# Attention scores with keys on partitions, no row maximum, and the old program kept behind a branch

## The chip, the cores and the metric

The kernel runs on one core of a Trainium2 chip. The core has a matrix engine (TensorE; its matmuls are called PE and its weight loads PEld in the profile), a vector engine (VectorE, DVE), a scalar engine (ScalarE, ACT), a general engine (GpSimd, POOL) and a queue engine (SyncE, SP) which starts the DMAs here. Each runs its own list of instructions in order, and semaphores hold one back until another has delivered. SBUF is the memory on chip, of 128 partitions; matmuls write to PSUM. The metric is the device time of one execution in microseconds (us), lower is better.

## What is computed

```python
# q, k, v: (4, 8, 768, 64), proj: (64, 6), w_in: (512, 2048), w_out: (2048, 512), alpha: (2048,)
q_bits = (np.einsum('bhsd,dk->bhsk', q, proj) > 0)      # the same for k
q_bucket = np.sum(q_bits * 2 ** np.arange(6), axis=-1)  # the same for k
mask = q_bucket[:, :, :, None] == k_bucket[:, :, None, :]
scores = scale * np.matmul(q, k.transpose(0, 1, 3, 2))
scores = np.where(mask, scores, -1000000000.0)
scores = scores - np.max(scores, axis=-1, keepdims=True)
attn = np.exp(scores)
attn = attn / (np.sum(attn, axis=-1, keepdims=True) + 1e-09)
x = (attn @ v).transpose(0, 2, 1, 3).reshape(3072, 512)
h = x @ w_in
g = np.maximum(h, 0.0) + alpha * np.minimum(h, 0.0)
out = g @ w_out
```

q, k and v are normal numbers times 0.1. The weights come as float64 and are rounded to float32 on chip. A query without any key in its bucket attends to all keys alike.

## The kernel before

Heads go in pairs, one on partitions 0 to 63, the other on 64 to 127; there are 4 batches of 4 pairs. A step (`scores`, L188) takes 128 queries of a pair against all 768 keys. The queries are on partitions. A bf16 matmul of the hash bits (`kb`, `qb`) puts 0 where the buckets are equal and a large negative number elsewhere, and the fp32 matmul of `kT` and `qT` adds the scores onto it in PSUM (L195). VectorE clamps the row and takes its maximum (L204, L207), ScalarE takes the exponentials and their sum (L209), and GpSimd divides by the sum (L219). The product with v needs the weights with keys on partitions, so `turn_probs` (L222) turns them on TensorE, 128 by 128 at a time (tile `pp`, L229), ScalarE copies them back (`pt`, L233), and `attend` (L235) multiplies with v (L242).

A batch has 24 steps, the program 96. The first 16 steps also each round one of sixteen half weight tiles (`round_weight`, L141: two passes on ScalarE, five on VectorE, L151 to L159, one on GpSimd, L158), loaded two ahead into two buffers. From step 26 on the MLP of the batch before is spread between the steps (`mlp_slice`, L288): `ff1` (L251, tile `h`, then two VectorE operations into `g`) and `ff2` (L265, tile `z`). The last batch's MLP runs alone after the attention has ended. A step turns, hashes and prepares the next pair as well (`turn`, L164; `hash_bits`, L175). The engines' lists follow this order, except that the scheduler moves an instruction forward where the operands of the next one in its list are late. An fp32 matmul stands as one row in the order and as two passes, each with a weight load of its own, in the profile.

PSUM has 8 banks: two for `tp`, used by all small products, two for `ff`, and two for the scores of each head.

Of the kernel before, what the change touches and what calls it, by code (L numbers as in the profile page):

```python
# [8 lines left out]
F32 = mybir.dt.float32  # L9
BF16 = mybir.dt.bfloat16  # L10
# [6 lines left out]
def kernel(  # L17
# [11 lines left out]
    """Hash-bucketed attention, then the PReLU MLP, all in float32.  # L29

    Heads go in pairs (head A on partitions 0-63, head B on 64-127). Token 6p + c of a
    sequence sits at column 128c + p throughout, so that loads and stores have long runs.
    Queries lie on partitions for the softmax; the weights are turned on the tensor
    engine, and v^T @ P^T gives x already transposed for the first MLP product.

    Bucket mask: with bits in {0, 1},
        sum_i (qb_i - 1/2) * 2*BIG*kb_i - BIG*qb_i = -BIG * (number of unequal bits),
    a matmul of powers of two that is exactly 0 for equal buckets. The scores are added
    onto it in PSUM, and max(., CLAMP) makes every masked entry the reference's -1e9
    (before the scale), so a row without any equal bucket becomes uniform as there.  # L40

    The MLP weights come as float64 bits; they are rounded to float32 on chip.
    """
# [18 lines left out]
    HI_MIN = 2.0 ** -15                                 # bits 0x38000000: 2^-127 as a float64's upper half  # L62
    HI_MAX = (2.0 - 2.0 ** -3 - 2.0 ** -23) * 2.0 ** 16  # bits 0x47EFFFFF: just below 2^128
# [77 lines left out]
    def round_weight(i):  # L141
        """hi, lo: the halves of a float64. Its exponent is moved to float32's range by
# [92 lines left out]
    def attend(pi, g):  # L235
# [4 lines left out]
        for kc in range(NC):  # L240
            for s in range(2):
# [3 lines left out]
                )  # L245
        nc.vector.tensor_copy(xT[b][:, hp, g * 2 * P : (g + 1) * 2 * P], ps)  # L246

# [1 line left out]
    gT, z, mpool = {}, {}, []  # L249

    def ff1(b, ch, f):  # L251
# [124 lines left out]
```

## Time and profile before

| | |
|---|---|
| median of 3 runs | 1307.92 us (1305.82 to 1308.66) |
| the profiled execution, span | 1303.8 us |
| granted TensorE clock, mean | 0.975 |
| HBM read, written | 35.67 MB, 6.29 MB |

In the profile, a group is one line's instructions of one kind: what they write and read, the shape, how many, the busy time and the mean of one, then the idle time of the engine just before them and what ended it. "64*128" is the part of the array that a matmul or a weight load takes, in rows and columns. Matmuls overlap with the next, so that the spacing of their starts tells what one costs, and not its mean length.

### The profile page before, as it was taken

How to read it: one execution, taken by the hardware profiler on the slowest of the kernel's cores; microseconds unless marked ns; L12 is line 12 of the kernel's file. 1: busy time of each engine (PE TensorE's matmuls, PEld its weight loads, DVE VectorE, ACT ScalarE, POOL GpSimd, SP SyncE). 2: the span in 40 equal slices, each digit the busy share in tenths (PEclk: the TensorE clock that was granted, in tenths of full speed). 3: DMA queues.
4: the chain of work that ended last, by engine and by line, in shares of the span. 5: the costliest groups of instructions: out<-in, count | busy, mean ns of one | idle time of the engine just before them, and what ended most of it. 6: DMA issues, size and time to landing. Idle time of an engine off the chain costs nothing.

```text
span 1303.8 us, 14044 instructions
## 1 busy us (share of the span) xinstructions
PE 1247.5 (96%) x5569; PEld 669.4 (51%) x5569; DVE 516.0 (40%) x1140; ACT 414.5 (32%) x793; POOL 222.8 (17%) x214
## 2 busy tenths in 40 slices
PE   6778899999999999999999999999999999999998
PEld 3444455555545555555555554555545555554553
DVE  5877654454215432244223442244323441040230
ACT  3665545433223323233232332323323233100000
POOL 2643532211111111111111111111111111000000
PEclk8997789999999999999999999999999999999999
DMA  8343301101010010101001010100000000000000
GB/s 216 111 156 107 122 13 37 37 1 37 9 34 19 1 37 17 45 1 25 21 9 45 1 37 9 41 13 13 1 17 9 1 1 9 17 1 16 9 0 25
DMA packets 62755, 42.87 MB, mean 33 GB/s; under 512 B 51408, under 2 KB 55520, under 8 KB 62688
## 3 DMA queue, kind: packets, MB, share of 16 engines
q1 hardware_dynamic: 62688, 41.97, 11.1%
q8 instruction: 44, 0.72, 0.2%
q14 instruction: 23, 0.19, 0.0%
HBM read 35.67 MB, written 6.29 MB: 32 GB/s over the span
## 4 chain that ended last, share of the span: by engine, by line
PE 74%; DVE 12%; ACT 7%; issue 3%; POOL 2%; SPq 1%; DMA 0%; ACTq 0%; POOLq 0%; DVEq 0%
PE z L271 26%; PE h L255 15%; PE sc L195 12%; PE av L242 9%; PE pp L229 7%; DVE pr L204 7%; ACT pr L209 5%; ACT pt L233 2%; PE hs_k L181 2%; PE hs_q L181 1%; POOL wr L158 1%; POOL pr L219 1%; DVE nm L207 1%; PE tp_k L172 1%; DVE wr L156 1%
## 5 line engine op out<-in xcount | busy, mean ns | idle before, releaser
L255 PE MATMUL h<-xT,w_in 128*128 128x384 f32 x1024 | 361.2, 492 | 0.0
L271 PE MATMUL z<-w_out,g 128*128 128x512 f32 x768 | 349.8, 597 | 0.0
L209 ACT ACTIVATE pr<-pr,nm 128x768 f32<-128x768 f32 x192 | 178.0, 928 | 500.0 <-DVE nm L207 500.0
L219 POOL TENSOR_SCALAR pr<-pr,rs 128x768 f32<-128x768 f32 x192 | 184.8, 974 | 809.4 <-DVE rs L217 529.9
L204 DVE TENSOR_SCALAR_CACHE_REDUCE pr<-sc 128x768 f32<-128x768 f32 x192 | 176.6, 953 | 188.5 <-PE sc L195 188.5
L255 PEld LDWEIGHTS h<-xT,w_in 128*128 128x128 f32 x1024 | 184.2, 190 | 117.5 <-issue 14.6
L271 PEld LDWEIGHTS z<-w_out,g 128*128 128x128 f32 x768 | 139.3, 190 | 152.7 <-issue 148.2
L229 PEld LDWEIGHTS pp<-ident,pr 128*128 128x128 f32 x1152 | 134.6, 144 | 131.8 <-ACT pt L233 60.1
L229 PE MATMUL pp<-ident,pr 128*128 128x128 f32 x1152 | 170.0, 284 | 33.5 <-ACT pt L233 15.8
L233 ACT COPY pt<-pp 128x512 f32<-128x512 f32 x288 | 158.4, 582 | 97.2 <-PE pp L229 96.0
L195 PE MATMUL sc<-kT,qT 64*128 64x512 f32 (+1 forms) x768 | 185.0, 509 | 0.0
L260 DVE TENSOR_SCALAR neg<-h,alpha 128x384 f32<-128x384 f32 x128 | 79.1, 618 | 227.6 <-PE h L255 227.5
L242 PE MATMUL av<-pt,vn 128*64 128x256 f32 x1152 | 138.8, 388 | 2.8 <-ACT pt L233 2.8
L242 PEld LDWEIGHTS av<-pt,vn 128*64 128x64 f32 x1152 | 79.8, 139 | 48.8 <-ACT pt L233 9.2
L195 PEld LDWEIGHTS sc<-kT,qT 64*128 64x128 f32 x768 | 77.9, 198 | 42.0 <-issue 39.1
L195 PE MATMUL sc<-kb,qb 64*128 64x256 bf16 (+1 forms) x384 | 79.7, 339 | 8.2 <-DVE pr L204 7.8
L277 ACT COPY o<-z 128x512 f32<-128x512 f32 x24 | 13.9, 580 | 220.0 <-PE z L271 220.0
L246 DVE COPY xT<-av 128x256 f32<-128x256 f32 x48 | 20.3, 422 | 152.2 <-PE av L242 152.1
L262 DVE SCALAR_TENSOR_TENSOR g<-h,neg 128x384 f32<-128x384 f32 x128 | 71.4, 558 | 4.3
L195 PEld LDWEIGHTS <-qb 64*128 64x128 bf16 x384 | 22.4, 94 | 85.0 <-issue 83.9
L216 DVE TENSOR_SCALAR rs<-rs 128x2 f32<-128x2 f32 x96 | 19.2, 200 | 93.3 <-ACT pr L209 92.6
L158 POOL TENSOR_TENSOR wr<-wx,wr 128x1024 f32<-128x1024 f32 x16 | 37.7, 2354 | 74.8 <-ACT wx L150 22.2
(46 smaller groups left out, 415.1 us busy)
## 6 DMA issues: line engine op xcount, KB each, us to landing
raw<-in_moe_w_in_dram SPq DMA_DIRECT2D x8, 1024.0 KB, 5.2
raw<-in_moe_w_out_dram SPq DMA_DIRECT2D x8, 1024.0 KB, 5.0
qn<-in_q_dram SPq DMA_DIRECT2D x32, 192.0 KB, 3.4
kn<-in_k_dram SPq DMA_DIRECT2D x32, 192.0 KB, 3.3
vn<-in_v_dram SPq DMA_DIRECT2D x16, 384.0 KB, 3.1
out_dram<-o SPq DMA_DIRECT2D x24, 256.0 KB, 2.0
wq<-in_proj_dram SPq DMA_DIRECT2D x2, 1.5 KB, 3.2
wk<-in_proj_dram SPq DMA_DIRECT2D x2, 1.5 KB, 2.1
```

The source lines that it names most:

```text
L158: nc.gpsimd.tensor_tensor(r, x, r, op=ALU.add)
L195: nc.tensor.matmul(sc[s][:, lo:hi], what["q", pi][r, qs], what["k", pi][r, lo:hi], start=first, stop=not first,)
L204: nc.vector.tensor_scalar(pr[:, s], sc[s], CLAMP, None, op0=ALU.max, op1=ALU.max, accum_out=mx[:, s : s + 1],)
L209: nc.scalar.activation(pr[:, s], pr[:, s], AF.Exp, scale=SCALE, bias=nm[:, s : s + 1], accum_out=rs[:, s : s + 1],)
L219: nc.gpsimd.tensor_scalar(pr[:, s], pr[:, s], rs[:, s : s + 1], 1.0, op0=ALU.mult, op1=ALU.mult)
L229: nc.tensor.transpose(ps[:, kk, j * P : (j + 1) * P], prob[pi, 2 * g + j][:, s, (kc + kk) * P : (kc + kk + 1) * P], ident,)
L233: nc.scalar.copy(p[:, kc : kc + 2], ps)
L242: nc.tensor.matmul(ps[D * s : D * s + D], nat["v", pi][:, s, kc * D : (kc + 1) * D], pt[pi, g, s][:, kc], start=(kc == 0), stop=(kc == NC ...
L255: nc.tensor.matmul(ps, w[:, kk, o : o + P], xT[b][:, kk, ch * CW : (ch + 1) * CW], start=(kk == 0), stop=(kk == NK - 1),)
L260: nc.vector.tensor_scalar(neg, ps, 0.0, alpha[:, f : f + 1], op0=ALU.min, op1=ALU.mult)
L262: nc.vector.scalar_tensor_tensor(g, ps, 0.0, neg, op0=ALU.max, op1=ALU.add)
L271: nc.tensor.matmul(ps, gT[b, ch, f][:, t * P : (t + 1) * P], w_out[part][:, i], start=(f == 0), stop=(f == NF - 1),)
```

## The change

The old function is kept, under the name `general_path`. A new `fast_path` runs first and writes the whole output. It also writes a flag, which all five engines read at the end; where it isn't 0, `general_path` computes everything again.

In `fast_path` a unit is 384 queries of a pair, 32 units in all, in four slots each. `scores` takes 128 keys as the stationary operand and 384 queries as the moving one, for both heads into two PSUM banks, so the exponentials come out with keys on partitions. They aren't turned, and no row maximum is taken. `hash_bits` is one product with 64 columns for q and one for k, side by side, and the bits lie on 12 rows of each head in place of 64. The bits' constant is 2^20 in place of 2^34 and the clamp is left out, so that masked entries come out of the exponential as 0. The sum over keys is made by adding the six tiles of exponentials (`acc`), five additions on GpSimd, in the first four pairs the last two of them on VectorE, and by a product with a matrix of ones (`sm`). `attend` multiplies with undivided exponentials; tiles carry a 385th column of ones, with which the mean of v falls out. `divide` multiplies by the reciprocal, and puts the mean of v where the sum is 0. `magnitude` takes the largest and smallest entries of q^T and k^T, and `verdict` makes the flag from them. Two weights are rounded in a unit (8 units), and the MLP starts with unit 9. The `ff1`, `ff2`, `round_weight` and the loads are as before, except that `g` has 18 buffers and not 20.

```diff
-def tile_hash_attn__then__act_prelu_kernel(
+def general_path(
...
+    flag = const_flag = None
+    args = (tc, q, k, v, proj, moe_w_in, moe_w_out, moe_alpha, out)
+    keep = ctx.enter_context(tc.tile_pool(name="keep", bufs=1))
+    flag = keep.tile([1, 1], mybir.dt.int32, name="flag")
+    fast_path(*args, flag)
+    again = tc.nc.values_load(flag[0:1, 0:1])
+    with tc.If(again > 0):
+        general_path(*args)
...
+    BIG = 2.0 ** 20
+    SAFE = 80.0 / SCALE / D
...
+    NPT = 9
+    pts = [const.tile([P, 2, CW + 1], F32, name=f"pt{i}") for i in range(NPT)]
...
+    def turn(pi, name, half):
+        src = nat[name, pi].rearrange("p c h d -> p c (h d)")
+        if half == 0:
+            tr[name, pi] = pool.tile([P, S], F32, name=f"{name}T{pi}", tag=f"{name}T")
+        ps = psum.tile([P, CW], F32, name=f"tp_{name}{pi}{half}", tag="mi")
+        for i in range(CH):
+            nc.tensor.transpose(ps[:, i * P : (i + 1) * P], src[:, CH * half + i], ident)
+        nc.scalar.copy(tr[name, pi][:, half * CW : (half + 1) * CW], ps)
+    def magnitude(pi, name):
+        n = "qk".index(name)
+        for i, op in enumerate((ALU.max, ALU.min)):
+            nc.vector.tensor_reduce(
+                mags[:, n, 2 * pi + i : 2 * pi + i + 1], tr[name, pi], axis=mybir.AxisListType.X, op=op,
+            )
+    def hash_bits(pi, half):
+        if half == 0:
+            for name in "qk":
+                bits[name, pi] = pool.tile([P, S], BF16, name=f"{name}b{pi}", tag=f"{name}b")
+        cols = slice(half * CW, (half + 1) * CW)
+        ps = psum.tile([P, CW], F32, name=f"hs{pi}{half}", tag="mi")
+        for n, name in enumerate("qk"):
+            nc.tensor.matmul(ps[D * n : D * n + D], wh, tr[name, pi][:, cols], start=True, stop=True)
+        for s in range(2):
+            dst = slice(D * s, D * s + 2 * NB)
+            r = slice(32 * s, 32 * s + 2 * NB)
+            nc.vector.tensor_scalar(bits["q", pi][dst, cols], ps[r], 0.0, cq[r], op0=ALU.is_gt, op1=ALU.subtract)
+            r = slice(D + 32 * s, D + 32 * s + 2 * NB)
+            nc.vector.tensor_scalar(bits["k", pi][dst, cols], ps[r], tk[r], mk[r], op0=ALU.is_gt, op1=ALU.mult)
+    def scores(pi, g, part):
+        qs = slice(g * CW, (g + 1) * CW)
+        for kc in (2 * part, 2 * part + 1):
+            sc = psum.tile([P, 2, 512], F32, name=f"sc{pi}_{g}_{kc}", tag="sc")
+            ks = slice(kc * P, (kc + 1) * P)
+            for what, first, rows in ((bits, True, 2 * NB), (tr, False, D)):
+                for s in range(2):
+                    r = slice(D * s, D * s + rows)
+                    nc.tensor.matmul(
+                        sc[:, s, :CW], what["k", pi][r, ks], what["q", pi][r, qs], start=first, stop=not first,
+                    )
+            pt = pts[n_pt[0] % NPT]
+            n_pt[0] += 1
+            nc.scalar.activation(pt[:, :, :CW], sc[:, :, :CW], AF.Exp, scale=SCALE)
+            prob[pi, g, kc] = pt
+            if kc == 1:
+                acc[pi, g] = pool.tile([P, 2, CW], F32, name=f"acc{pi}_{g}", tag="acc")
+            if kc >= 1:
+                a = acc[pi, g]
+                first = prob[pi, g, 0][:, :, :CW] if kc == 1 else a
+                eng = nc.vector if pi < NP and kc >= 4 else nc.gpsimd
+                eng.tensor_tensor(a, first, pt[:, :, :CW], op=ALU.add)
+    def attend(pi, g):
+        ps = psum.tile([P, CW + 1], F32, name=f"av{pi}_{g}", tag="mi")
+        for kc in range(NC):
+            for s in range(2):
+                nc.tensor.matmul(
+                    ps[D * s : D * s + D], nat["v", pi][:, s, kc * D : (kc + 1) * D], prob[pi, g, kc][:, s],
+                    start=(kc == 0), stop=(kc == NC - 1),
+                )
+        if g == 0:
+            vmean[pi] = pool.tile([P, 1], F32, name=f"vm{pi}", tag="vm")
+            nc.vector.tensor_scalar(vmean[pi], ps[:, CW : CW + 1], 1.0 / S, None, op0=ALU.mult)
+        raw_x = pool.tile([P, CW], F32, name=f"rx{pi}_{g}", tag="rx")
+        nc.scalar.copy(raw_x, ps[:, :CW])
+        av[pi, g] = raw_x
+    def divide(pi, g):
+        b, hp = pairs[pi]
+        if hp == 0 and g == 0:
+            xT[b] = pool.tile([P, NP, S], F32, name=f"xT{b}", tag="xT")
+        ps = psum.tile([P, CW], F32, name=f"sm{pi}_{g}", tag="mi")
+        for s in range(2):
+            nc.tensor.matmul(ps[D * s : D * s + D], ones, acc[pi, g][:, s], start=True, stop=True)
+        den = pool.tile([P, CW], F32, name=f"dn{pi}_{g}", tag="dn")
+        alone = pool.tile([P, CW], F32, name=f"al{pi}_{g}", tag="al")
+        x = xT[b][:, hp, g * CW : (g + 1) * CW]
+        nc.vector.tensor_scalar(alone, ps, 0.0, vmean[pi], op0=ALU.is_equal, op1=ALU.mult)
+        nc.vector.tensor_scalar(den, ps, 1e-36, None, op0=ALU.max)
+        nc.vector.reciprocal(den, den)
+        nc.gpsimd.tensor_tensor(den, av[pi, g], den, op=ALU.mult)
+        nc.gpsimd.tensor_tensor(x, den, alone, op=ALU.add)
...
+        g = mpool[0].tile([P, CW], F32, name=f"g{b}_{ch}_{f}", tag="g", bufs=NF + 2)
...
+    def verdict():
+        both = const.tile([P, 2, 2], F32, name="both")
+        for i, op in enumerate((ALU.max, ALU.min)):
+            nc.vector.tensor_reduce(
+                both[:, :, i], mags.rearrange("p n (x t) -> p n x t", t=2)[:, :, :, i],
+                axis=mybir.AxisListType.X, op=op,
+            )
+        top = const.tile([P, 2], F32, name="top")
+        nc.vector.tensor_scalar(both[:, :, 1], both[:, :, 1], -1.0, None, op0=ALU.mult)
+        nc.vector.tensor_tensor(top, both[:, :, 0], both[:, :, 1], op=ALU.max)
+        row = const.tile([1, 2], F32, name="row")
+        for n in range(2):
+            ps = psum.tile([1, P], F32, name=f"vd{n}", tag="mi")
+            nc.tensor.transpose(ps, top[:, n : n + 1], ident)
+            nc.vector.tensor_reduce(row[:, n : n + 1], ps, axis=mybir.AxisListType.X, op=ALU.max)
+        nc.vector.tensor_tensor(row[:, 0:1], row[:, 0:1], row[:, 1:2], op=ALU.mult)
+        nc.vector.tensor_scalar(row[:, 0:1], row[:, 0:1], SAFE, None, op0=ALU.is_le)
+        nc.vector.tensor_scalar(flag, row[:, 0:1], -1.0, 1.0, op0=ALU.mult, op1=ALU.add)
+    UNITS = NP * NCH
+    SLOTS = 4 * UNITS
+    total = NPAIR * NCH
+    def mlp_slice(u, slot):
+        n = 4 * (u - UNITS - 1) + slot
+        if n < 0:
+            return
+        b, i = divmod(n, SLOTS)
+        if b < B:
+            m = mlp[b]
+            for fn, *a in m[len(m) * i // SLOTS : len(m) * (i + 1) // SLOTS]:
+                fn(*a)
+    def ahead(u, slot):
+        pi, g = divmod(u, NCH)
+        if pi + 1 >= NPAIR:
+            return
+        if slot < 2:
+            turn(pi + 1, "qk"[g], slot)
+        elif slot == 2:
+            magnitude(pi + 1, "qk"[g])
+        if g == 1 and slot >= 2:
+            hash_bits(pi + 1, slot - 2)
+    weights = ctx.enter_context(ExitStack())
+    wpool = weights.enter_context(tc.tile_pool(name="wstage", bufs=2))
+    NW = 2 * len(views)
+    load_qk(0)
+    setup()
+    load_v(0)
+    load_qk(1)
+    for name in "qk":
+        for half in range(2):
+            turn(0, name, half)
+        magnitude(0, name)
+    for half in range(2):
+        hash_bits(0, half)
+    setup_alpha()
+    load_v(1)
+    load_weight(0)
+    load_weight(1)
+    for u in range(total + UNITS + 2):
+        pi, g = divmod(u, NCH)
+        live = u < total
+        if u == UNITS:
+            weights.close()
+            mpool.append(ctx.enter_context(tc.tile_pool(name="mlp", bufs=2)))
+        for slot in range(4):
+            if live and slot != 1:
+                scores(pi, g, (0, None, 1, 2)[slot])
+            if live and slot == 0 and g == 0 and pi + 2 < NPAIR:
+                load_qk(pi + 2)
+                load_v(pi + 2)
+            if slot % 2 == 0 and 2 * u + slot // 2 < NW:
+                i = 2 * u + slot // 2
+                round_weight(i)
+                if i + 2 < NW:
+                    load_weight(i + 2)
+            if live:
+                ahead(u, slot)
+            mlp_slice(u, slot)
+            if 0 < u <= total:
+                before = divmod(u - 1, NCH)
+                if slot == 0:
+                    attend(*before)
+                if slot == 2:
+                    divide(*before)
+        if u == total + 1:
+            verdict()
```

TensorE in the mixed stage before, one step of the first MLP batch (`h` is the MLP, `sc` the scores, `pp` the turned probabilities):

```order
L195 LDWEIGHTS qb_1547
L195 MATMUL sc_3_0_1849<-kb_1596,qb_1547 128x512
L195 LDWEIGHTS qb_1547
L195 MATMUL sc_3_1_1850<-kb_1596,qb_1547 128x512
L195 MATMUL sc_3_0_1849<-kT_1478,qT_1425 128x512
L172 MATMUL tp_k_1826<-ident,kn_1347 128x128 x3
L172 MATMUL tp_k_1831<-ident,kn_1347 128x128 x3
L195 MATMUL sc_3_1_1850<-kT_1478,qT_1425 128x512
```

And after, in the mixed stage, between two pieces of the MLP (`sm` is the product that makes the sums; `kb` and `qb` are the bits):

```order
L632 MATMUL h_1_11_2047<-xT_387,w_in_79 128x384 x4
L615 MATMUL sm_1_2056<-acc_1_1798,ones 64x384 x2
L578 LDWEIGHTS kb_1872
L578 MATMUL sc_0_4_2066<-qb_1871,kb_1872 128x384
L578 LDWEIGHTS kb_1872
L578 MATMUL sc_0_4_2066<-qb_1871,kb_1872 128x384
L578 MATMUL sc_0_4_2066<-qT_1685,kT_1800 128x384 x2
L578 LDWEIGHTS kb_1872
L578 MATMUL sc_0_5_2073<-qb_1871,kb_1872 128x384
L578 LDWEIGHTS kb_1872
L578 MATMUL sc_0_5_2073<-qb_1871,kb_1872 128x384
L578 MATMUL sc_0_5_2073<-qT_1685,kT_1800 128x384 x2
```

Keys have become the weights. For each tile of 128 keys the list goes from the bits' 12 rows to the scores' 64 rows and back. Over the whole list the shape of the array changes 599 times in the fast path, 192 of them from a 32-row shape to a 64-row one and 100 straight back; before it changes 362 times.

VectorE in the rounding stage before (`wx`, `wr`, `w_in` belong to a weight, `pr` and `mx` to the row maxima, `nm` and `rs` to the softmax's factors):

```order
L183 TENSOR_SCALAR qb_389<-hs_q_393,cq 128x384
L152 TENSOR_SCALAR wx_419<-wx_419 128x1024
L216 TENSOR_SCALAR rs_4_413<-rs_4_413 128x2
L204 TENSOR_SCALAR pr_5_471,mx_5_472<-sc_5_0_461 128x768
L155 TENSOR_SCALAR wr_420<-wx_419 128x1024
L217 RECIPROCAL rs_4_413<-rs_4_413 128x2
L204 TENSOR_SCALAR pr_5_471,mx_5_472<-sc_5_1_462 128x768
L156 SCALAR_TENSOR_TENSOR wr_420<-raw_286,wr_420 128x1024
```

And after (`mags` are the magnitudes, `al` and `dn` the steps of `divide`):

```order
L526 TENSOR_SCALAR wr_442<-wx_441 128x1024
L526 TENSOR_SCALAR wr_494<-wx_493 128x1024
L527 SCALAR_TENSOR_TENSOR wr_442<-raw_320,wr_442 128x1024
L527 SCALAR_TENSOR_TENSOR wr_494<-raw_374,wr_494 128x1024
L530 SCALAR_TENSOR_TENSOR w_in_79<-raw_320,wr_442 128x1024
L530 SCALAR_TENSOR_TENSOR w_in_79<-raw_374,wr_494 128x1024
L548 TENSOR_REDUCE mags<-qT_453 128x1 x2
L619 TENSOR_SCALAR al_1_511<-sm_1_507,vm_341 128x384
L620 TENSOR_SCALAR dn_1_510<-sm_1_507 128x384
L591 TENSOR_TENSOR acc_0_431<-acc_0_431,pt_92 128x768
L621 RECIPROCAL dn_1_510<-dn_1_510 128x384
L591 TENSOR_TENSOR acc_0_431<-acc_0_431,pt_93 128x768
```

Row maxima and two-column factors have left the queue; two weights are now rounded side by side, and magnitudes, additions and a reciprocal of 384 columns stand between the weights.

More of the change, by code (lines that the diff above doesn't have):

```diff
@@ L345, with kernel @@
         mlp_slice(step, 1)
+@with_exitstack
+def kernel(
+    ctx: ExitStack,
+    tc: tile.TileContext,
+    q: bass.AP,
+    k: bass.AP,
+    v: bass.AP,
+    proj: bass.AP,
+    moe_w_in: bass.AP,
+    moe_w_out: bass.AP,
+    moe_alpha: bass.AP,
+    out: bass.AP,
+):
+    flag = const_flag = None
[6 more added lines that the diff above has]
+        general_path(*args)
```

153 lines of the change are left out of this document (152 added, 1 removed).

## The prediction

> **What bounds the kernel now.** I read the page first, then the busy time by stages (each row: its stretch in us and its length; then busy us of PE, PEld, DVE, ACT and POOL with instruction counts; granted clock; DMA share; GB/s), then the chain that ended last.
>
> ```profile
> span 1303.8 us, 14044 instructions
> PE 1247.5 (96%) x5569; PEld 669.4 (51%) x5569; DVE 516.0 (40%) x1140; ACT 414.5 (32%) x793; POOL 222.8 (17%) x214
> 0.00:14.00 14.00, 7.39 (x23) 4.15 (x25) 3.91 (x24) 3.20 (x5) 0.70 (x6) 1.00 0.72 159
> 14.00:177.20 163.20, 134.69 (x605) 69.20 (x604) 124.76 (x208) 91.47 (x150) 77.51 (x46) 0.80 0.42 131
> 177.20:242.00 64.80, 61.26 (x386) 35.05 (x387) 29.17 (x83) 37.41 (x76) 19.64 (x22) 1.00 0.10 25
> 242.00:1135.10 893.10, 879.18 (x4111) 476.26 (x4110) 320.54 (x762) 278.33 (x555) 124.95 (x140) 1.00 0.06 18
> 1135.10:1303.80 168.70, 164.94 (x448) 84.75 (x447) 37.61 (x64) 4.09 (x7) 0.00 (x0) 1.00 0.03 11
> 270.62 3.87 PE h L255 x12
> 421.40 3.87 PE h L255 x12
> 1217.56 41.28 PE h L255 x128
> 1258.84 41.21 PE z L271 x96
> ```
>
> There are four stages. From 14.0 to 177.2 sixteen half weight tiles are rounded beside attention steps; VectorE is busy 124.76 of 163.2 us there, more than any engine but TensorE, whose busy time is stretched by a clock of 0.80 and by waits. To 242 attention runs alone. To 1135 attention and MLP share a TensorE that is busy 98% of the time, while DVE has 36% and ACT 31%. The last 165 us are MLP alone. A pass of 384 columns takes 41.28/128 = 0.3225 us, one of 512 takes 41.21/96 = 0.429. In the third stage the chain meets the same work at 270.62 and 421.40, twelve steps apart: 150.8 us, or 12.57 a step. So this stage is priced by TensorE's stream, and the second by VectorE's queue.
>
> **The steady stage, by TensorE.** One step of before, in order of time (start, length, group):
>
> ```profile
> 576.00 0.39 PE L195 MATMUL sc<-kb,qb 64*128 64x512 bf16 x2
> 576.23 1.02 PE L195 MATMUL sc<-kT,qT 64*128 64x512 f32 x4
> 577.08 0.27 PE L195 MATMUL sc<-kb,qb 64*128 64x256 bf16 x2
> 577.19 0.60 PE L195 MATMUL sc<-kT,qT 64*128 64x256 f32 x4
> 577.72 2.85 PE L255 MATMUL h<-xT,w_in 128*128 128x384 f32 x8
> 580.40 1.04 PE L229 MATMUL pp<-ident,pr 128*128 128x128 f32 x8
> 583.02 2.81 PE L242 MATMUL av<-pt,vn 128*64 128x256 f32 x24
> 585.76 2.20 PE L255 MATMUL h<-xT,w_in 128*128 128x384 f32 x6
> L229 PE MATMUL pp<-ident,pr 128*128 128x128 f32 x1152 | 170.0, 284 | 33.5 <-ACT pt L233 15.8 <-POOL pr L219 11.5 <-DVE qb L183 3.2
> ```
>
> Starts give the real spacing. Four fp32 score passes (two heads, two passes each) of 512 columns take 576.23 to 577.08, 0.85 us: the heads run side by side at 0.43 a pair. A bf16 pair costs 0.23 for 512 and 0.11 for 256, so 0.16 for 384. Twelve av pairs of 256 take 2.74. A transpose takes 0.88/8 = 0.109 (580.40 to the next group at 581.28). And each change of array shape costs: the four 256-column passes ought to take 0.43 but the next group starts after 0.53 (0.10); the eight h passes ought to take 2.58 and take 2.68 (0.10 more, the weight load that could not be loaded ahead). I count 0.2 into fp32 weights of 128 columns, 0.15 into 64 columns (from the 0.16 that av's 12 pairs take beyond 12 x 0.215), 0.1 into bf16.
>
> Check on before, per step: MLP 1024 x 0.3225 + 768 x 0.429 = 660 us over 96 steps, 6.87; scores 1.62; transposes of probabilities 12 x 0.109 = 1.31; av 1.29; hash 0.43; q and k transposes 0.22; sum 11.74. The order holds 362 changes of shape, 3.77 a step, some 0.57. Together 12.31 against 12.57 measured; 0.26 is left for waits, mostly for copies of P^T.
>
> After, per unit (half a head pair, the work of three steps): MLP 20.62; scores 6 x (0.16 + 2 x 0.3225) = 4.83; av 12 x 0.323 = 3.88; denominators 2 x 0.3225 = 0.65; hash 0.65, because q and k now take one half of the columns each and run side by side; q and k transposes 6 x 0.109 = 0.65. Sum 31.3, against 3 x 11.74 = 35.2. All 1152 transposes of probabilities are gone (125 us at 0.109), and hash halves. But the order of after holds 599 changes of shape. The bit matmuls use 12 rows, so a 32-row shape, and the scores a 64-row one; 192 times the array goes from the first to the second and 100 times straight back. At 195 x 0.2 + 115 x 0.2 + 196 x 0.1 + 93 x 0.15 = 95 us they are 3.0 a unit (before: 1.7). With 0.45 for waits, a unit is 34.7 us against 37.7.
>
> The prices between 32 and 64 rows are the uncertain ones. The trace has one such change:
>
> ```profile
> 13.30 0.13 PEld L122 LDWEIGHTS alps<-ident,alpha 16*128 16x128 f32 x1 [0.74 <-DVE kb L185]
> 13.46 0.09 PEld L195 LDWEIGHTS <-qb 64*128 64x128 bf16 x1
> 15.67 0.64 PEld L172 LDWEIGHTS tp_q<-ident,qn 128*128 128x128 f32 x6 [0.33 <-issue]
> 16.47 0.09 PEld L195 LDWEIGHTS <-qb 64*128 64x128 bf16 x1 [0.17 <-issue]
> ```
>
> The 64-row weights come 0.16 us after the 16-row load, though only 16 columns are streamed in between; from 128 rows the same load comes 0.80 us after the first of six transposes, that is 0.80 - 5 x 0.109 = 0.25 after the last, which streams 0.109. Both leave some 0.1 that no streaming fills, so I charge the change in full; the lower end is nothing. The Trainium skill, "TensorEngine Tiling (Array Packing)", section Tiling Modes, says that a change of mode drains the TensorE, whichever modes; by it the full charge stands and the sum is as above, without it the first rival's. One row agrees, and no long run of such changes is in this trace.
>
> **The rounding stage, by VectorE.** Its rows in that stage (busy us, mean ns), one of POOL and one of the smallest DVE operation:
>
> ```profile
> L156 DVE SCALAR_TENSOR_TENSOR wr<-raw,wr 128x1024 f32<-128x1024 uint32 x16 | 20.3, 1271 | 0.2
> L151 DVE TENSOR_SCALAR wx<-wx 128x1024 f32<-128x1024 f32 x16 | 14.0, 877 | 1.3 <-ACT wx L150 1.3
> L152 DVE TENSOR_SCALAR wx<-wx 128x1024 uint32<-128x1024 uint32 x16 | 13.4, 838 | 0.2
> L155 DVE TENSOR_SCALAR wr<-wx 128x1024 uint32<-128x1024 uint32 x16 | 11.7, 729 | 0.4
> L159 DVE SCALAR_TENSOR_TENSOR w_out<-raw,wr 128x1024 uint32<-128x1024 uint32 x8 | 10.6, 1329 | 6.7 <-POOL wr L158 6.7
> L159 DVE SCALAR_TENSOR_TENSOR w_in<-raw,wr 128x1024 uint32<-128x1024 uint32 x8 | 10.5, 1309 | 11.6 <-POOL wr L158 11.6
> L204 DVE TENSOR_SCALAR_CACHE_REDUCE pr<-sc 128x768 f32<-128x768 f32 x32 | 29.8, 946 | 5.3 <-PE sc L195 5.3
> L183 DVE TENSOR_SCALAR qb<-hs_q,cq 128x384 bf16<-128x384 f32 x6 | 3.6, 608 | 0.4 <-PE hs_q L181 0.4
> L217 DVE RECIPROCAL rs<-rs 128x2 f32<-128x2 f32 x15 | 2.4, 158 | 0.1
> L158 POOL TENSOR_TENSOR wr<-wx,wr 128x1024 f32<-128x1024 f32 x16 | 37.7, 2354 | 74.8 <-ACT wx L150 22.2 <-DVE wr L156 18.8 <-ACT wx L157 15.8
> L115 DVE MEMSET cq<- 128x1 f32 x1 | 0.1, 59 | 0.0
> ```
>
> Before, DVE spends 124.76/16 = 7.80 us a weight. After, a unit carries two weights: rounding 2 x 80.5/16 = 10.06; two magnitude reductions of 768 columns at 0.946 (nearest row, L204) = 1.89; four bit operations of 384 columns at 0.61 = 2.43; two additions at 1.271 x 768/1024 = 1.91 (the row with two streams); `alone`, `den` at 0.61 and the reciprocal of 384 columns. That one is not in the trace. Two columns take 0.158 against 0.059 for the smallest operation, so at most 0.05 a column, 20 us; at least it is another 384-column operation. I take 0.6, since beside the other small operations it shows no price per column. With 0.1 for vmean the sum is 18.2 us, 9.1 a weight. The row maxima (2 x 0.946 a step) are gone, but what replaces them fills the same queue, since 16 steps of attention become 24 (eight units). Scaled by the stage of before: 163.2 x 9.1/7.80 = 190 us. Bounds: DVE never idle, 8 x 18.2 = 146; a weight's chain never overlapped (ACT about 1.1, DVE 5.03, POOL 2.35, a load of about 5), 16 x 13.7 = 219.
>
> **The sum.** First scores at 14 + 4 x 0.946 + 4 x 0.61, the magnitudes and four more bit operations: 20. Rounding, 8 units: 190. One attention unit alone, 34.7 - 20.6: 14. 23 mixed units x 34.7: 798. One unit with only attention's last half: 20.6 + 3.9 + 0.7 + 0.7 = 26. MLP alone: 165. The last copy and store, as before 3.8 (1300.05 to 1303.8), and reading the flag and branching on five engines, of which the trace shows nothing: 4 (0 if the store's landing hides it, 10 if each of two jumps waits as long as a load of about 5 us). Span 1221. The median is 4.1 above the profiled span, so **1225**. The stage of rounding ends some 18 us sooner than 242 with a third more attention behind it; the mixed stage pays back the rest. ACT loses copies of P^T and gains one small copy; POOL has five additions at 2.354 x 0.75 and two halves, 10.6 of 34.7 us. The new wait is that of the denominator product (`sm`) for POOL's last addition; behind it on TensorE stand the scores of the next two key tiles. POOL has two slots, half of 34.7 us, for its last two additions of 1.8, so the wait stays covered; uncovered it costs such an addition, about 2 us a unit. The verdict's two transposes and few one-column operations stand in the MLP stage, below 1 us.
>
> **Rivals.** First, 32 and 64 rows change for nothing: (192 x 0.2 + 100 x 0.1)/32 x 23 = 35 us less, **1190**. Against it is the row at 13.46. Second, the reciprocal takes eight passes: at (946 - 59)/768 = 1.15 ns a column, 8 x 384 x 1.15 = 3.5 us, 2.9 more per unit on DVE; in the rounding stage 8 x 2.9 x 163.2/124.76 = 30, **1255**; the mixed stage hides it. The two-column row can't exclude it. The Trainium skill, "VectorE: DVE Perf Modes", section on the walkthrough of the 8-slice pipeline, gives the reciprocal's iterative divide a repeat count of 8; no run here shows it. Third, the slower side: the reciprocal costs the bound, 20 us. DVE then has 38 us a unit against TensorE's 14; 8 x 19.5 x 1.31 = 204, **1430**; it decides from 82/(8 x 1.31) = 7.8 us more, 0.022 us a column. That small operations on two columns cost alike speaks against it. Fourth, the rounding chain does not overlap: **1254**. Fifth, the flag sends the program down the old path as well: 1225 + 1304, about **2530**; the flag needs only values whose largest products stay under the bound, and q and k are drawn at a tenth of a normal.
>
> **How the numbers follow.** Forecast 0.47, first rival 0.12, second 0.26, third 0.03, fourth 0.10, fifth 0.01, no gain for reasons not seen 0.01. The range takes in the first, second and fourth rivals and, at its ends, the bounds of the rounding stage (44 less and 29 more), partly together: 1180 to 1275. Faster 0.95, same 0.01, slower 0.04; 0.2% is about what a measurement of this kernel tells from none.
>
> **What would show it.** Right: no pp group; period of a unit near 34.7 us with TensorE over 97% busy; score groups of 1.0 to 1.1 us per key tile; MLP starting near 224; DVE busiest before. Wrong: 0.8 us per key tile (first rival); a reciprocal over 3 us; TensorE idle on denominators in the mixed stage; any instruction of the old path.

## The result and the profile after

| | us | beside the kernel before |
|---|---|---|
| after, median of 4 | 1216.78 (1216.49 to 1218.48) | 0.9314 [0.9299, 0.933] |
| before, median of 4 on the same chip | 1306.87 | 1 |
| after, span of the profiled execution | 1215.0 | before 1303.8 |

The new kernel is 6.9% faster; 1225 was forecast. First the head of its page and the busy time by stages, with the columns of the prediction (stretch and its length; busy us of PE, PEld, DVE, ACT, POOL; granted clock; DMA share; GB/s).

```profile
span 1215.0 us, 10348 instructions
PE 1132.4 (93%) x4163; PEld 503.5 (41%) x4163; DVE 527.1 (43%) x697; ACT 243.3 (20%) x345; POOL 364.3 (30%) x239
0.00:14.00 14.00, 5.70 (x24) 3.18 (x24) 8.42 (x40) 3.20 (x5) 0.98 (x15) 0.95 0.82 205
14.00:214.40 200.40, 133.02 (x570) 48.26 (x569) 171.77 (x163) 80.27 (x103) 108.10 (x52) 0.77 0.36 109
214.40:238.00 23.60, 22.36 (x87) 7.71 (x88) 15.10 (x17) 7.00 (x10) 9.53 (x7) 0.72 0.13 33
238.00:1044.10 806.10, 806.10 (x3035) 359.45 (x3036) 293.44 (x410) 148.77 (x220) 245.73 (x166) 1.00 0.07 19
1044.10:1215.00 170.90, 165.22 (x451) 84.89 (x449) 38.33 (x69) 4.10 (x7) 0.00 (x0) 1.00 0.03 12
```

Then rows of the chain that ended last (start, length, engine and work):

```profile
588.34 7.06 PE z L648 x16
...
725.44 7.06 PE z L648 x16
...
1044.13 18.06 PE h L632 x56
```

The last weight tile is rounded at 214.4 us (177.2 before), beside eight units, the attention work of 24 steps where before it was 16. The MLP runs steadily from 238.3 (242 before); four of its passes stand alone at 205.1. The mixed stage then takes 806 us in place of 893, and the MLP alone 165, as before. So the start of the mixed stage gained 4 us and the stage itself 87. In that stage TensorE has no idle time in the records; the same `z` work comes at 588.34 and 725.44, four units apart, so a unit takes 137.1/4 = 34.28 us, where three steps of before took 37.7.

In the rounding stage VectorE is busy 171.77 of 200.4 us, 21.5 us a unit. Its largest groups there, and POOL's (shape, count, busy us, mean ns of one, idle time before them and what ended it):

```profile
L527 DVE SCALAR_TENSOR_TENSOR wr<-raw,wr 128x1024 f32<-128x1024 uint32 x16 | 22.2, 1400 | 0.1
L530 DVE SCALAR_TENSOR_TENSOR w_in<-raw,wr 128x1024 uint32<-128x1024 uint32 x8 | 19.6, 2457 | 13.8 <-POOL wr L529 13.8
L530 DVE SCALAR_TENSOR_TENSOR w_out<-raw,wr 128x1024 uint32<-128x1024 uint32 x8 | 18.8, 2353 | 12.3 <-POOL wr L529 12.3
L523 DVE TENSOR_SCALAR wx<-wx 128x1024 uint32<-128x1024 uint32 x16 | 18.4, 1166 | 0.1
L522 DVE TENSOR_SCALAR wx<-wx 128x1024 f32<-128x1024 f32 x16 | 17.1, 1081 | 1.3 <-ACT wx L521 1.2
L621 DVE RECIPROCAL dn<-dn 128x384 f32<-128x384 f32 x6 | 15.3, 2545 | 0.0
L526 DVE TENSOR_SCALAR wr<-wx 128x1024 uint32<-128x1024 uint32 x16 | 12.2, 778 | 0.1
L529 POOL TENSOR_TENSOR wr<-wx,wr 128x1024 f32<-128x1024 f32 x16 | 43.1, 2695 | 37.2 <-DVE wr L527 29.7 <-ACT pt L583 7.5
L591 POOL TENSOR_TENSOR acc<-acc,pt 128x768 f32<-128x768 f32 x16 | 32.6, 2036 | 7.2 <-ACT pt L583 6.9
```

Two things stand out. The reciprocal takes 2.55 us. And the last operation of a weight takes 2.4 us, with 26.1 us of waiting for POOL in front of the two groups; before, the same operation took 1.31 to 1.33 us, with 18.3 us of waiting. The other weight operations have lengthened too.

TensorE waits for this queue. Its longest waits between 14 and 238 us (for what, total, times, longest):

```profile
PE sc L578 <- DVE kb L567: 29.7, 4, 9.2
PE av L598 <- DVE dn L620: 24.2, 3, 8.4
```

The four waits for `kb`, the bits, stand before units 2, 4, 6 and 8, the first units of a pair, whose last bits VectorE makes near the end of the unit before. So a pair's first unit starts 26 to 39 us after the unit before it, and its second unit 15 to 18 us after the first.

### The profile page after: what moved, and what is told of

Same layout as the page of the kernel before. It is cut to its first block, busy times and chain, and to the rows that moved or that the text cites. A ratio compares the mean times of both kernels' runs of the same rounds, so it can differ in the third digit from the quotient of the medians.

```text
span 1215.0 us, 10348 instructions
## 1 busy us (share of the span) xinstructions
PE 1132.4 (93%) x4163; PEld 503.5 (41%) x4163; DVE 527.1 (43%) x697; ACT 243.3 (20%) x345; POOL 364.3 (30%) x239
## 4 chain that ended last, share of the span: by engine, by line
PE 84%; DVE 9%; POOL 3%; issue 3%; ACT 1%; DMA 0%; POOLq 0%; ACTq 0%
PE z L648 28%; PE h L632 27%; PE sc L578 14%; PE av L598 9%; POOL wr L529 3%; PE hs L561 2%; PE sm L615 2%; DVE wx L523 1%; DVE wr L527 1%; DVE wx L522 1%; DVE w_in L530 1%; PE tp_q L541 1%; PE tp_k L541 1%; DVE kb L567 1%; DVE w_out L530 1%
## 5 line engine op out<-in xcount | busy, mean ns | idle before, releaser
L591 POOL TENSOR_TENSOR acc<-acc,pt 128x768 f32<-128x768 f32 x112 | 193.6, 1729 | 447.2 <-ACT pt L583 444.0
L632 PEld LDWEIGHTS h<-xT,w_in 128*128 128x128 f32 x1024 | 189.4, 190 | 136.8 <-issue 14.8
L583 ACT ACTIVATE pt<-sc 128x768 f32<-128x768 f32 x192 | 154.9, 811 | 450.3 <-PE sc L578 450.3
L578 PE MATMUL sc<-qT,kT 64*128 64x384 f32 x768 | 188.8, 561 | 0.0
L598 PE MATMUL av<-pt,vn 128*64 128x385 f32 x768 | 142.4, 521 | 24.2 <-DVE dn L620 24.2
L578 PE MATMUL sc<-qb,kb 12*128 12x384 bf16 x384 | 70.7, 344 | 38.6 <-DVE kb L567 31.6
L591 POOL TENSOR_TENSOR acc<-pt,pt 128x768 f32<-128x768 f32 x32 | 59.3, 1853 | 120.6 <-ACT pt L583 120.6
L621 DVE RECIPROCAL dn<-dn 128x384 f32<-128x384 f32 x32 | 81.6, 2551 | 0.9
L578 PEld LDWEIGHTS sc<-qT,kT 64*128 64x128 f32 x768 | 61.5, 193 | 36.0 <-issue 36.0
L622 POOL TENSOR_TENSOR dn<-rx,dn 128x384 f32<-128x384 f32 x32 | 36.1, 1128 | 71.8 <-DVE dn L621 71.7
L565 DVE TENSOR_SCALAR qb<-hs,cq 12x384 bf16<-12x384 f32 x64 | 37.7, 590 | 37.6 <-PE hs L561 37.1
```

Of the source, the lines that this page charges most:

```text
L565: nc.vector.tensor_scalar(bits["q", pi][dst, cols], ps[r], 0.0, cq[r], op0=ALU.is_gt, op1=ALU.subtract)
L578: nc.tensor.matmul(sc[:, s, :CW], what["k", pi][r, ks], what["q", pi][r, qs], start=first, stop=not first,)
L583: nc.scalar.activation(pt[:, :, :CW], sc[:, :, :CW], AF.Exp, scale=SCALE)
L591: eng.tensor_tensor(a, first, pt[:, :, :CW], op=ALU.add)
L598: nc.tensor.matmul(ps[D * s : D * s + D], nat["v", pi][:, s, kc * D : (kc + 1) * D], prob[pi, g, kc][:, s], start=(kc == 0), stop=(kc == N ...
L621: nc.vector.reciprocal(den, den)
```

## The experiments

The questions: does the change between 12 and 64 rows of the array cost what the forecast charged; what lengthens the rounding stage, VectorE's own list (theory A) or the work on POOL beside it (theory B); and what do the branch and the magnitudes cost.

**One number of rows.** The bits go into fixed tiles that are zero outside their 12 rows, and the matmul takes all 64.

```diff
+    bit_tiles = [[const.tile([P, S], BF16, name=f"{name}b{i}") for name in "qk"] for i in range(2)]
...
+                nc.gpsimd.memset(t, 0.0)
...
-                bits[name, pi] = pool.tile([P, S], BF16, name=f"{name}b{pi}", tag=f"{name}b")
+                bits[name, pi] = bit_tiles[pi % 2][n]
...
-            for what, first, rows in ((bits, True, 2 * NB), (tr, False, D)):
+            for what, first, rows in ((bits, True, D), (tr, False, D)):
```

> The bits lie on 64 rows of each head again, the rows beyond the twelve filled with zeros, so that the bit matmul and the score matmul have one array shape; the four bit tiles are fixed and are set to zero once. Theory (a change between the 32-row and the 64-row shape drains the array and leaves a weight load uncovered, 0.2 us into the scores and 0.1 us back): a key tile falls from 1.11 us to 0.81 to 0.83 us within a block, a unit of the mixed stage from 34.28 us to about 32.8, and the whole by 23 x 1.5 = 35 us, to about 1182 us. Rival (the 1.11 us are the short bit matmuls themselves, too short to cover the loading of fp32 weights, whatever the shape): a key tile stays at 1.0 us or more and the whole within 8 us of 1217.

Measured: 1174.41 us, ratio 0.899 [0.8975, 0.9005], 42 us less than after. TensorE's records in time order, for two key tiles of a steady slot of after (start, length, group):

```profile
553.47 0.34 PE L578 MATMUL sc<-qb,kb 12*128 12x384 bf16 x2
553.74 0.92 PE L578 MATMUL sc<-qT,kT 64*128 64x384 f32 x4
554.59 0.34 PE L578 MATMUL sc<-qb,kb 12*128 12x384 bf16 x2
554.85 0.92 PE L578 MATMUL sc<-qT,kT 64*128 64x384 f32 x4
555.70 5.43 PE L632 MATMUL h<-xT,w_in 128*128 128x384 f32 x16
```

The same place in this run:

```profile
563.07 0.34 PE L582 MATMUL sc<-qb,kb 64*128 64x384 bf16 x2
563.24 0.81 PE L582 MATMUL sc<-qT,kT 64*128 64x384 f32 x4
563.89 0.33 PE L582 MATMUL sc<-qb,kb 64*128 64x384 bf16 x2
564.05 0.81 PE L582 MATMUL sc<-qT,kT 64*128 64x384 f32 x4
```

Read the starts. With 12 rows a key tile takes 553.47 to 554.59, 1.12 us; the bits take 0.27 of it and the scores 0.85. With 64 rows it takes 0.82: 0.17 and 0.65, which is the streaming alone. More rows of zeros cost nothing, and the two changes of shape cost 0.10 and 0.20 a key tile. The records of the bit pair itself last the same, 0.34 and 0.33 to 0.34; the time that is gone stood between the groups. The period of a unit falls from 34.28 to 32.76 us, 1.52; over 23.5 units that is 36, as the theory has it (35). The steady MLP starts at 231.2, 7 us sooner, which the theory left out. Of these, 1.9 are the rounding, whose last weight is done at 212.5, and some 1.8 the changes of unit 8 (6 x 0.30). The rest, over 3 us, goes with the granted clock: after the last weight it was 0.50 until 227.5 us in the kernel after and until 218 here, then 0.99 in both, and the same product with v takes 5.47 us in the first and 4.10 in the second. So the charge was real, and some 3 of the 42 us aren't its doing.

**No reciprocal.** `divide` multiplies by the sums themselves.

```diff
-        nc.vector.reciprocal(den, den)
```

> The reciprocal of the denominators is left out, so that the output is multiplied by the sum and not divided by it. Theory A (the rounding stage is set by the length of VectorE's queue): 8 units lose 2.55 us each, the stage shrinks by 15 to 21 us, the whole is about 1199 us; the mixed stage stays at 34.3 us a unit. Theory B (the stage is set by the chain of each weight through VectorE, GpSimd and the next load): the whole shrinks by less than 6 us.

Measured: 1202.6 us, 0.9196 [0.9172, 0.922]; 14.2 less than after. The last weight is rounded 15.5 us sooner (198.9), and the period is still 34.28. VectorE's list sets the rounding stage, as theory A has it (15 to 21 in the stage; the whole gained a little less); and outside that stage the reciprocal is hidden.

**The rounding's addition on VectorE.** 

```diff
-        nc.gpsimd.tensor_tensor(r, x, r, op=ALU.add)
+        nc.vector.tensor_tensor(r, x, r, op=ALU.add)
```

> The one addition of the weight rounding that GpSimd makes is made by VectorE. Theory A (the rounding stage is set by the length of VectorE's queue, whose operations cost what they cost alone): 16 additions of 1024 columns at about 1.2 us make the stage 16 to 20 us longer, the whole about 1235 us. Theory B (VectorE loses more by waiting for that addition, 26 us of idle time before the last rounding step, and by running beside it, 1.23 us stretched to 2.4 us sixteen times): the stage gets 15 to 30 us shorter, the whole is about 1195 us.

Measured: 1202.02 us, 0.9219 [0.9187, 0.925]; 14.8 less, the period unchanged. The stage to the last weight, in the columns of the stages above:

```profile
14.00:200.00 186.00, 139.27 (x571) 50.11 (x569) 178.11 (x177) 80.04 (x103) 70.25 (x36) 0.79 0.38 119
```

VectorE's new group in it:

```profile
L529 DVE TENSOR_TENSOR wr<-wx,wr 128x1024 f32<-128x1024 f32 x16 | 26.8, 1684 | 1.8 <-ACT wx L528 1.8
```

VectorE takes over sixteen additions, 26.8 us by its own record, and is busy only 6.3 us longer in total, 178.11 against 171.77. The rest of its list got shorter by some 20 us, and its idle time fell from 28.6 to 7.9. This is theory B's outcome, just under its 15 to 30. With the run before it, both theories hold a part: VectorE is the queue, and POOL's work beside it stretches and stalls that queue.

**No branch.** The flag is computed, nobody reads it, and the old program isn't in the kernel.

```diff
-    again = tc.nc.values_load(flag[0:1, 0:1])
-    with tc.If(again > 0):
-        general_path(*args)
```

> The flag is still computed but not read, and the old program is left out of the kernel. Theory (reading the flag and branching lengthens the end alone: 5.7 us from the last matmul to the end of the span, 3.8 us before the change): the whole is 2 us shorter, about 1215 us. Rival (the longer program or the check costs in the middle as well): more than 5 us shorter.

Measured: 1215.8 us (1212.91 to 1216.79), 0.9303 [0.9285, 0.9321]. By the whole time the 1.0 us cannot be told from none. The trace can tell it, by the issue of the last store (start, length). In after, whose span ends at 1215.0:

```profile
1210.01 0.34 SPq L655 DMA_DIRECT2D out_dram<-o  x1
```

In this run, which ends at 1214.1:

```profile
1211.03 0.34 SPq L652 DMA_DIRECT2D out_dram<-o  x1
```

In before, which ends at 1303.8:

```profile
1300.73 0.33 SPq L278 DMA_DIRECT2D out_dram<-o  x1
```

From that issue to the end it is 4.99, 3.07 and 3.07 us. Reading the flag and branching cost 1.9 us.

**No magnitudes.** The reductions of q^T and k^T are gone, and the flag is made from zeros.

```diff
-                nc.vector.tensor_reduce(
-                    mags[:, n, 2 * pi + i : 2 * pi + i + 1], tr[name, pi], axis=mybir.AxisListType.X, op=op,
-                )
+        if pi == 0:
+            nc.gpsimd.memset(mags[:, n], 0.0)
```

> The changed kernel without the magnitude reductions: the check is left out, the flag is made from zeros. Theory (what the rounding stage pays is VectorE's queue; without the reciprocals 2.55 us a unit less brought 14 us, 0.7 us for each microsecond of queue): 1.89 us a unit less make the whole 9 to 13 us shorter, about 1206 us, and the mixed stage stays at 34.3 us a unit. Rival (reductions run where VectorE would wait for the weight's addition anyway): within 3 us of 1217.

Measured: 1207.2 us, 0.9243 [0.9223, 0.9262]; 9.6 less, the last weight at 206.2 in place of 214.4, the period unchanged. As expected (9 to 13): the guard costs some two thirds of what VectorE spends on it while it rounds (16 reductions of 0.94, 14.8 us), and nothing in the mixed stage.

**Both of the edits that help.** The 64 rows and the rounding's addition on VectorE together; the next runs build on this one.

```diff
-            for what, first, rows in ((bits, True, 2 * NB), (tr, False, D)):
+            for what, first, rows in ((bits, True, D), (tr, False, D)):
...
-        nc.gpsimd.tensor_tensor(r, x, r, op=ALU.add)
+        nc.vector.tensor_tensor(r, x, r, op=ALU.add)
```

> The two edits that helped together: bits on 64 rows, and the weights' addition on VectorE. Theory (one acts in the mixed stage on TensorE, the other in the rounding stage on VectorE, and they are independent): 1174 - 15 = about 1160 us. Rival (they share a gain, since a shorter TensorE list helps the rounding stage too): 1165 to 1172 us.

Measured: 1157.85 us, 0.8856 [0.8841, 0.8871]; 58.9 less than after, against 42.4 + 14.8 = 57.2 apart. The two do not touch each other: one is TensorE's stream, the other VectorE's queue.

**All additions of the sums on POOL.** The last two additions of a unit, which VectorE makes in the first four pairs, go to POOL as well.

```diff
-                eng = nc.vector if pi < NP and kc >= 4 else nc.gpsimd
+                eng = nc.gpsimd
```

> As the run of both edits, and the sums of exponentials are added on GpSimd alone in the first four pairs too. Theory (VectorE's queue sets the stage and GpSimd has room since the weights' additions have left it): 2 us a unit less on VectorE, at 0.7, make it 10 to 13 us shorter than the run of both edits. Rival (GpSimd beside VectorE stretches VectorE's operations by about what it takes off): within 4 us of it.

Measured: 1174.52 us, 0.8978 [0.896, 0.8996]. That is 16.7 us **longer** than the run before it, and both expectations failed. The stage to the last weight in the run before:

```profile
14.00:193.60 179.60, 119.79 (x571) 52.52 (x570) 176.11 (x177) 79.84 (x103) 72.49 (x36) 0.81 0.40 124
```

Two of VectorE's groups in it:

```profile
L527 DVE TENSOR_SCALAR wx<-wx 128x1024 uint32<-128x1024 uint32 x16 | 18.0, 1140 | 0.1
L534 DVE SCALAR_TENSOR_TENSOR w_in<-raw,wr 128x1024 uint32<-128x1024 uint32 x8 | 10.2, 1290 | 0.0
```

The stage here:

```profile
14.00:212.10 198.10, 115.67 (x570) 51.37 (x567) 190.93 (x163) 78.45 (x103) 103.27 (x52) 0.81 0.36 111
```

The two groups here:

```profile
L527 DVE TENSOR_SCALAR wx<-wx 128x1024 uint32<-128x1024 uint32 x16 | 23.2, 1462 | 0.2
L534 DVE SCALAR_TENSOR_TENSOR w_in<-raw,wr 128x1024 uint32<-128x1024 uint32 x8 | 18.1, 2268 | 0.1
```

VectorE has 14 instructions less in this stage and is busy 14.8 us longer. The same operations have stretched: 1.29 to 2.27 us, 1.14 to 1.46. One such operation in the timeline of this run (start, length):

```profile
98.49 2.00 POOL L595 TENSOR_TENSOR acc<-acc,pt 128x768 f32<-128x768 f32 x1
98.88 2.69 DVE L534 SCALAR_TENSOR_TENSOR w_in<-raw,wr 128x1024 uint32<-128x1024 uint32 x1
```

POOL's addition ends at 100.49; VectorE's operation ends at 101.57, 1.08 us later, close to the 1.21 that it takes alone. It looks as if it had stood still until POOL was done, while its record counts as busy. Not every operation stretches: in the two runs the reductions stay at 0.94, the bits at 0.68 and 0.60 to 0.61, the reciprocal at 2.54. So a new theory: an addition on POOL takes its time from VectorE's weight operations as well.

**No additions on POOL.** It was tested by taking the cause away: the run with both edits, where POOL's three additions of a unit are left out in the first four pairs. VectorE's list stays the same.

```diff
-            if kc >= 1:
+            if kc >= (4 if pi < NP else 1):
...
-                first = prob[pi, g, 0][:, :, :CW] if kc == 1 else a
+                first = prob[pi, g, 0][:, :, :CW] if kc == (4 if pi < NP else 1) else a
```

> The run of both edits, with GpSimd's three additions a unit left out in the first four pairs: there the sum over keys is of three tiles of six. VectorE's list is the same, operation for operation. Theory (GpSimd's additions stretch the VectorE operations that run beside them): VectorE's weight operations go back to their lengths alone, about 0.69, 0.69, 0.68, 1.2, 1.2 and 1.23 us, 27 us in 16 weights and 15 additions, and the whole is 18 to 27 us below 1158. Rival (their lengths come from transfers or from ScalarE): within 5 us of 1158.

Measured: 1133.27 us, 0.8675 [0.8659, 0.8692]; 24.6 less than with them. Its stage:

```profile
14.00:168.80 154.80, 112.29 (x571) 49.68 (x571) 151.93 (x177) 79.75 (x103) 16.09 (x12) 0.86 0.46 144
```

The two groups in it:

```profile
L527 DVE TENSOR_SCALAR wx<-wx 128x1024 uint32<-128x1024 uint32 x16 | 11.7, 746 | 0.1
L534 DVE SCALAR_TENSOR_TENSOR w_in<-raw,wr 128x1024 uint32<-128x1024 uint32 x8 | 9.6, 1213 | 0.0
```

With and without them VectorE is busy 98% of the stage, on the same 177 instructions: 176.11 us and 151.93. Its records are shorter by 24.2 us, the total by 24.6. The 24 additions on POOL cost VectorE 1.0 us each. The price isn't the same for every addition: in the run with all of them on POOL, VectorE lost 14 records of 1.2 us and was still busy 14.8 longer, so the 16 further ones cost it some 2 us each, as much as they last. What decides how much of an addition VectorE pays wasn't isolated.

**Additions on VectorE instead.** In the run with both edits four of a unit's five additions go to VectorE, in the first four pairs.

```diff
-                eng = nc.vector if pi < NP and kc >= 4 else nc.gpsimd
+                eng = nc.vector if pi < NP and kc >= 2 else nc.gpsimd
```

> The run of both edits, with four of five additions of a unit on VectorE in the first four pairs, and one on GpSimd. Theory (an addition on GpSimd takes about as much of VectorE's time as making it there, 17 us for 16 additions in the run with all on GpSimd): two more on VectorE, 16 x 0.9 = 14 us of queue, give back about the same in shorter neighbours, so the whole stays within 6 us of 1158. Rival (only the length of VectorE's list counts): 10 to 14 us longer.

Measured: 1155.01 us, 0.884 [0.8822, 0.8857]; 2.8 less than with both edits, with overlapping intervals. For these additions it hardly matters where they stand: one costs VectorE some 0.93 us in its own queue (7.6 + 7.2 us for 16 in the run without POOL's) and 1.0 as a neighbour.

**Another pace.** The last two weights are rounded in units 7 and 8, one in each, so that unit 8 isn't without them. Once in the run with all additions on POOL, once in the run with both edits.

```diff
+    PACE = [2] * 7 + [1, 1]
...
-        if u == UNITS:
+        if u == UNITS + 1:
...
-            if slot % 2 == 0 and 2 * u + slot // 2 < NW:
-                i = 2 * u + slot // 2
+            if slot % 2 == 0 and u < len(PACE) and slot // 2 < PACE[u]:
+                i = sum(PACE[:u]) + slot // 2
```

> As the run with the sums on GpSimd alone, and the last two weights are rounded one in unit 7 and one in unit 8, not both in unit 7. Unit 8 has attention only and an idle VectorE. Theory: the stage before the MLP loses most of one weight's time of 10 us, 4 to 9 us. Rival: the MLP's start then waits for the last weights, no gain.

> The run of both edits, with the last two weights rounded in unit 7 and unit 8. Theory: as with the sums on GpSimd, where it brought 12 us, about 1147 us. Rival (the longer stage there was what made room): within 4 us of 1158.

Measured: 1162.84 us, 0.8902 [0.8874, 0.893], 11.7 less than without it (4 to 9 expected); and 1153.64 us, 0.8835 [0.8817, 0.8853], 4.2 less, just beyond the "within 4" of the rival and far from the theory's 1147. It looks as if the pace helps by what VectorE's queue ran over, much where the stage was long, little where it wasn't; that wasn't tested by itself. The interval of the 4.2 us step overlaps that of the run without it.

**All that helped.** Both edits, four additions on VectorE, and the pace.

```diff
+    PACE = [2] * 7 + [1, 1]
...
-                eng = nc.vector if pi < NP and kc >= 4 else nc.gpsimd
+                eng = nc.vector if pi < NP and kc >= 2 else nc.gpsimd
```

> Four of five additions on VectorE in the first four pairs, and the last two weights in units 7 and 8: both edits that were a little below 1158. Theory (they act at different places): about 1150 us. Rival (a longer VectorE list leaves unit 8 nothing to give): 1153 to 1156 us.

Measured: 1149.62 us (5 executions, 1149.04 to 1150.75), 0.8795 [0.8783, 0.8807], as the theory has it (1150). Of the runs that compute the whole output this is the fastest, 67 us below the change.

## Why the prediction was right, and where a size was off

The forecast was 1225, its range 1180 to 1275, and 1216.78 came. The reason was the right one: TensorE's stream pays in the mixed stage, and VectorE's queue sets the rounding stage. That the sum came within 8 us is partly luck: the start of the mixed stage came 14 us late, and the mixed stage was 18 shorter. The terms, in us:

| term | predicted | measured |
|---|---|---|
| first exponentials | 20 | 15.7 |
| rounding, units 0 to 7 | 190 | 204.4 |
| unit 8 alone, MLP start | 14, at 224 | 16.8, and 1.4 to the steady `h` at 238.3 |
| mixed stage with the half unit | 798 + 26 = 824 | 806 |
| MLP alone | 165 | 165 |
| last matmul to the end | 7.8 | 5.7 |
| median above span | 4.1 | 1.8 |

- **The steady unit held**: 34.28 against 34.7. A key tile took 1.12 against 0.16 + 0.2 + 0.645 + 0.1 = 1.1. The first rival, changes of shape for nothing (1190), fell; the run with 64 rows, padding in place of changes, took out 1.52 us a unit, where the rival's working has (192 x 0.2 + 100 x 0.1)/32 = 1.5. The Trainium skill, "TensorEngine Tiling (Array Packing)", section Tiling Modes, says that a change of mode drains the TensorE; this trace agrees, and gives 0.10 us for the change without fp32 weights behind it.
- **The mixed stage was 18 shorter than the sum**: 23 units at 34.28 are 788 (10 less than 798), and what remains is 17 where the half unit was put at 26. The period is lower by 0.42; that is close to the 0.45 charged for waits, and TensorE shows no idle time there. Of the 9 us at the ends some 4 lie ahead of 238.3: the four `h` passes at 205.1, and of unit 9 two key tiles and three transposes. The rest isn't explained.
- **Unit 8 took 16.8 and not 14**: TensorE's granted clock was 0.50 until 227.5 us, and the sum took its times from stretches at full clock.
- **The rounding stage was mis-sized by 14**, from two terms of VectorE's list that were too small and a scale that was too large. The reciprocal was taken at 0.6, "since beside the other small operations it shows no price per column"; it took 2.55. From 2 columns (0.158) and 384 it has a price: (2551 - 158)/382 = 6.3 ns a column. Rival 2 put it at 3.5 and was nearer. The weights were taken over at 80.5/16 = 5.03 us of VectorE each; they took 6.8 (22.2 + 19.6 + 18.8 + 18.4 + 17.1 + 12.2 = 108.3 for 16), beside a POOL that now has the additions of the sums too; in the run without those additions, and with the weights' own on VectorE, the same six groups take 73.9 for 16. A unit came to 171.77/8 = 21.5 in place of 18.2; the two terms would make it 23.6, but the window holds six of the eight reciprocals, and records overlap a little. Against it, the scale 163.2/124.76 was too careful: VectorE came to 171.77/200.4 = 86% busy, not 76%. With the measured list and the old scale the stage would have been put at 225, with the old list and the measured share at 170: two errors of some 35 and 20 to 25 us, which partly cancelled. In the bound of an unoverlapped chain the four addends make 13.5 and not 13.7, 216 us in place of 219, which decides nothing.
- **Rival 2 (1255)** was right that the reciprocal has a price per column and that the mixed stage hides it, and too high on both prices: eight passes aren't borne out (6.3/1.15 is 5.5 of them), and the whole reciprocal of 2.55 us is worth 14 us, where it charged 30 for 2.9 us. The Trainium skill's "VectorE: DVE Perf Modes", section on the walkthrough of the 8-slice pipeline, has a repeat count of 8; at the 1.15 ns a column of the prediction that would be an estimate of 9.2 ns, and the trace has 6.3, which decides.
- **Rival 3 (20 us, 1430)** fell: it needed 8.4 us, and 2.55 came.
- **Rival 4 (no overlap, 1254)** fell for the whole: the stage is 204, not 219. Yet its kind of cost is there: 26.1 us of VectorE's idle time ends on POOL's addition, and moving that addition away saved 14.8.
- **The new wait stayed covered**: TensorE is busy 806.10 of 806.10 us in the mixed stage, and the only recorded idle time before `sm` is one of 5.9 us while the weights are rounded, so `sm` waited for no addition of POOL there.
- **The guard**: the magnitudes cost 9.6 us, all ahead of the mixed stage; the branch 1.9 and not 4; and no instruction of the old program ran, 10348 in all against 14044, so rival 5 fell.

What stays open: what the missing transposes are worth by themselves, since no run puts them back and only the sum of the stream carries their price; and how the wait for POOL (moving the addition takes it away) and the stretch (fewer additions) share the 14.8 us.

## What to carry to other kernels

Price a TensorE stream by its changes of array shape as well as by its columns: here a short contraction was filled with zero rows to the row count of its neighbour, which cost nothing and saved 1.5 us a unit. Where one engine's queue sets a stage, add up what the new work costs that queue, and look for one duration of each new operation at two sizes before taking it as cheap. Work moved to GpSimd isn't free for VectorE: compare the mean duration of VectorE's unchanged operations before and after, since here the time for which an operation was held up stands in its record as busy.

## What the runs showed of the hardware

- **An addition on POOL and the weight operations of VectorE beside it largely take turns.** The last operation of a weight takes 1.21 us where POOL has almost nothing to do and 2.3 to 2.6 beside POOL's additions; those take 2.04 on average in the rounding stage, and 1.67 where one starts first. In the timeline of the change itself:

```profile
130.30 1.67 POOL L591 TENSOR_TENSOR acc<-acc,pt 128x768 f32<-128x768 f32 x1
130.37 2.68 DVE L530 SCALAR_TENSOR_TENSOR w_out<-raw,wr 128x1024 uint32<-128x1024 uint32 x1 [2.24 <-POOL wr L529]
```

  POOL ends at 131.97, VectorE at 133.05, 1.08 later. The Trainium skill, "SBUF — State Buffer", section "SBUF: two separate sides", says that GpSimd shares a port pair with those operations of VectorE that run in a two-port mode or read two inputs from SBUF, that the one that starts first holds it for its whole instruction, and that the other blocks. The two timelines, whose VectorE operation reads two inputs from SBUF, and the run without POOL's additions agree with that; the 1.0 us that one of 24 additions cost there is less than the time an addition lasts.
- **The reciprocal is an operation of some 6.3 ns a column** between 2 and 384 columns, 2.55 us for 384, where a reduction of 768 columns takes 0.94.
- **Zero rows are free for TensorE**: a bf16 pair on 64 rows takes 0.17 us for 384 columns, against the 0.16 that the prediction counts for streaming alone.
